# Sixty-four tokens at a time: re-tiling a delta-rule recurrence that runs beside a feed-forward

## The chip, the cores and the metric

One Trainium2 chip, of which the kernel uses one core. The metric is device time in microseconds (us): the median of repeated executions. The engines are named as in the profile: PE (matmul) with PEld (its weight loads), DVE (vector), ACT (scalar), POOL, and SP, whose queue issues the DMAs. Each engine works through its own queue in the order in which the program issued the instructions.

## The reference, cut to what matters

A delta-rule attention over 4 batches, 8 heads, 768 tokens and a head size of 48, followed by a feed-forward with SiLU (384 to 2048 to 384) on the 3072 tokens.

```python
k_n = k / (np.linalg.norm(k, axis=-1, keepdims=True) + 1e-06)
state = np.zeros((B, H, D, D))
for t in range(S):
    kt, vt, bt = k_n[:, :, t], v[:, :, t], beta[:, :, t, None]
    y[:, :, t] = np.einsum('bhd,bhde->bhe', q[:, :, t], state)
    v_old = np.einsum('bhde,bhd->bhe', state, kt)
    state = state + bt[:, :, :, None] * np.einsum('bhd,bhe->bhde', kt, vt - v_old)
x = y.transpose(0, 2, 1, 3).reshape(B * S, H * D)
h = x @ w_in
out = (h * (1 / (1 + np.exp(-h)))) @ w_out
```

The weights arrive as 64-bit floats and are narrowed to 32 bits on the chip.

## The kernel before, in words

**Chunks and units.** The 768 tokens are cut into 6 chunks of 128. A unit is one batch of one chunk: 128 tokens on the 128 partitions, all 8 heads beside one another. So a chunk has four units.

**Attention of a chunk** has three parts.

- `prepare` (L889): for each unit, `turn` (L353) transposes keys and queries (tile `kq`, groups `pt`), and `score` (L376) multiplies keys with keys and with queries (L387, banks `pa`, 128x128 per head); ACT (L397) and DVE (L403, with the mask `above`) scale and mask the result into `ap`. `block_out` and `block_in` bring the 32x32 diagonal blocks of `ap` through DRAM into the tile `g`, one block to a partition. `scale` and `size` are POOL's work on keys and values.
- `invert` (L441): DVE inverts all 32x32 blocks of a chunk at once, two instructions for each of 30 steps (L465, L469); the inverses go through DRAM into `xe` and `xi`.
- `solve` (L508): `merge` (L526) makes inverses of 64x64 from those of 32x32. `keys` (L551) subtracts from the values what the state holds for the keys. `inner`, `across` (L567, L577) solve first for tokens 0 to 63 (partitions `lo`), then carry over to tokens 64 to 127 (`hi`), then solve these; `keep` copies results to `z`. `old` (L600) and `new` (L627) add up the output of old state and new tokens in a bank `pyc`, `update` (L609) adds to the state. Every batch has a state tile, moved once per chunk. Four units run through these steps as a pipeline, shifted by one. The output leaves a bank by copies of ACT and DVE in turn (L681) and, for odd heads, through the tile `part` and DMAs into `xT`.

**Feed-forward of a chunk** runs for two batches at a time (256 tokens): `hidden` (L724) is `xT` times `w_in` (L730, banks `phid`) with SiLU by ACT into `gT` (L740); then, for the first chunk, `project` (L748) multiplies with `w_out` (L753, `po`), and for the others `combine` (L810) does so with seven smaller products (L824, `px` and `py`) on sums of operands that DVE makes (`sum_g`, `sum_w`). It is a generator: every `go(pieces)` emits one piece, 1.3 to 1.5 us of matmuls.

**What sets the order.** `pin` (L88) fixes the order on each engine to the order of emission, `in_line` (L98) that of the DMAs on SP. The driver at the end of the kernel interleaves by hand: pieces of the feed-forward of chunk c are emitted between the steps of preparation, inversion and solution of chunk c + 1. `squares` and `norms` (L284, L301) make the next chunk's scale factors on ACT and DVE during `solve`.

**The start.** Nothing overlaps chunk 0's attention but the narrowing of the weights, 8 pieces of `w_in` and 8 of `w_out`: `narrow` (L150) has two steps on ACT (L158, L163), three on DVE (L160, L166, L170) and one on POOL (L174) for a piece. `fill(n)` emits n of the DVE steps, `until(piece)` all up to a piece. `busy` (L261) emits filler matmuls that touch nothing.

Of the kernel before, what the change touches and what calls it, by code (L numbers as in the profile page):

```python
# [21 lines left out]
def kernel(  # L22
# [84 lines left out]
    N = len(units)  # L107
    NK = NBK = NZ = B
# [9 lines left out]
    def chunk_of(src, i):  # L118
        b, c = units[i]
        return src[b, :, c * C : (c + 1) * C, :].rearrange("h t d -> t h d")  # L120

    def load_k(i):
        if i < N:
            in_line(nc.sync.dma_start(out=packed(kbufs[i % NK]), in_=chunk_of(k, i)))

    def load_q(i):
        if i < N:
            in_line(nc.sync.dma_start(out=packed(zbufs[i % NZ]), in_=chunk_of(q, i)))

    def load_v(i):  # L130
        if i < N and i not in vfs:
            vfs[i] = load.tile([P, H, D], FP32, name="vf", bufs=4)
            in_line(nc.sync.dma_start(out=vfs[i][:], in_=chunk_of(v, i)))
# [5 lines left out]
    states = [const.tile([P, NP, 2 * W], FP32, name=f"state{b}") for b in range(B)]  # L139
    pin(nc.vector.memset(states[B - 1][:], 0.0))  # L140
    beta_fm = mlp.tile([BH, S], FP32, name="beta_fm", tag="gT", bufs=3)
    in_line(nc.sync.dma_start(out=beta_fm[:], in_=beta.rearrange("b h s -> (b h) s")))
    for load_one in (load_k, load_q):
        for i in range(B):
            load_one(i)
# [107 lines left out]
    for t in states[: B - 1]:  # L253
        nc.gpsimd.memset(t[:], 0.0)

    HH = HB * H
# [4 lines left out]
    def busy(after=None, how=NoSync):  # L261

        pw = bank(psC, "c", "pw")
        done = pin(nc.tensor.matmul(
            pw[:, 0:DM], lhsT=ident[:],
            rhs=states[B - 1][:].rearrange("p a w -> p (a w)")[:, 0:DM], start=True, stop=True,
        ))
        if after is not None:
            behind(done, after, how)
        return done  # L270
# [5 lines left out]
    def beta_of(c):  # L276
        pb = bank(psA, "a", "pb")
        pin(nc.tensor.transpose(pb[:, 0:BH], beta_fm[:, c * C : (c + 1) * C], ident[0:BH, 0:BH]))
        pin(nc.scalar.activation(out=beta_tok[:, c, :], in_=pb[:, 0:BH], func=ACTF.Copy))
# [4 lines left out]
    def squares(c):  # L284

        sums[c] = small.tile([P, BH], FP32, name="ss", bufs=1)[:]
        for b in range(B):
            if c == 1:
                sq = packed(zbufs[b])
            else:  # L290
                if b % HB == 0:
                    two = work.tile([P, HB, H, D], FP32, name="sq", tag="g" if c > 0 else "xg"[b // HB], bufs=1)
                sq = two[:, b % HB]
            pin(nc.scalar.activation(
                out=sq, in_=packed(kbufs[(c * B + b) % NK]), func=ACTF.Square
            ))
            pin(nc.vector.tensor_reduce(
                out=sums[c][:, b * H : (b + 1) * H], in_=sq, axis=AX.X, op=ALU.add
            ))
# [45 lines left out]
    def size(i):  # L345
# [3 lines left out]
            out=vfs[i][:], in0=vfs[i][:],  # L349
# [25 lines left out]

    def score(i, u, rooms):  # L376

        b, c = units[i]
        kq, bt = u["kq"], steps[c][:, b * H : (b + 1) * H]
        ap = work.tile([P, H, 2, C], FP32, name="ap", tag="ap", bufs=4)  # L380
        u["ap"] = ap
        for g, room in enumerate(rooms):
            pa = [bank(*room, f"pa{e}") for e in range(2)]
            for pp in range(2):
                for e in range(2):
                    rows = slice(W * e, W * e + D)
                    u["last"] = pin(nc.tensor.matmul(  # L387
                        pa[e][:, pp * 2 * C : (pp + 1) * 2 * C],
                        lhsT=kq[rows, 2 * g + pp, 0, :],
                        rhs=kq[rows, 2 * g + pp, :, :].rearrange("p j t -> p (j t)"),  # L390
                        start=True, stop=True,
                    ))
            for e in range(2):
                heads = [(4 * g + 2 * pp + e, 2 * C * pp) for pp in range(2)]
                by_act = 2 - e
                for h, at in heads[:by_act]:
                    copied = pin(nc.scalar.activation(  # L397
                        out=ap[:, h, 0, :], in_=pa[e][:, at : at + C], func=ACTF.Copy,
                        scale=bt[:, h : h + 1],
                    ))  # L400
                for n, (h, at) in enumerate(heads):
                    j = 1 if n < by_act else 0
                    masked = pin(nc.vector.scalar_tensor_tensor(  # L403
                        out=ap[:, h, j:2, :],
                        in0=pa[e][:, at + j * C : at + 2 * C].rearrange(
                            "p (j t) -> p j t", j=2 - j
                        ),
                        scalar=bt[:, h : h + 1],
                        in1=above[:].unsqueeze(1).to_broadcast([P, 2 - j, C]),
                        op0=ALU.mult, op1=ALU.mult,  # L410
                    ))
            u["ends"] = (copied, masked)
            yield

    def block_out(i, u):
# [13 lines left out]
        for j in range(NB):  # L429
            rows = slice(T * j, T * (j + 1))  # L430
            in_line(nc.sync.dma_start(
                out=there[b, :, j].rearrange("h s t -> s h t"), in_=ap[rows, :, 0, rows]
# [8 lines left out]
    def invert(c):  # L441
# [41 lines left out]
        if c == 0:  # L483
            xe = sum_room[:, B * SLAB : B * SLAB + BH * T]
# [23 lines left out]
    def solve(c, us):  # L508
# [3 lines left out]
        lo, hi = slice(0, W), slice(W, P)  # L512
        A, CC = (psA, "a"), (psC, "c")
        vs = {x: vfs.pop(c * B + x) for x in range(B)}
        pzs, pys = {}, {}
        xe = xes.pop(c)

        def z_of(x):
            return zbufs[x]

        if c == 0:
            pin(nc.gpsimd.memset(sum_room[:, 0 : B * SLAB], 0.0))
            slab = {x: sum_room[:, x * SLAB : (x + 1) * SLAB] for x in range(B)}
        y = work.tile([P, 2, HH, T], FP32, name="y", tag="g", bufs=1)

        def merge(g, second):  # L526
# [3 lines left out]
            for n in range(HB):  # L530
                x = g * HB + n
                for h in range(H):
                    for k in range(2):
                        even, odd = slice(W * k, W * k + T), slice(W * k + T, W * (k + 1))
                        if second:
                            to, left, right = even, y[odd, g, n * H + h, :], xis[g][odd, n * H + h, T:W]
                        else:
                            to, left, right = odd, us[x]["ap"][even, h, 0, odd], xe[even, x * H + h, :]
                        at = T * (n * H + h)
# [4 lines left out]
            if second:  # L544
                pin(nc.scalar.copy(xis[g][0:T, :, T:W], pm[0:T]))
                pin(nc.vector.tensor_copy(out=xis[g][W : W + T, :, T:W], in_=pm[W : W + T]))
            else:
                pin(nc.scalar.copy(y[T:W, g], pm[T:W]))
                pin(nc.vector.tensor_copy(out=y[W + T : P, g], in_=pm[W + T : P]))

        def keys(x):  # L551

            ph = bank(*CC, "ph")
            for p in range(NP):
                st = states[x][:, p, :].rearrange("p (e w) -> p e w", e=2)[:, :, 0:D]
                pin(nc.tensor.matmul(  # L556
                    ph[:, 2 * D * p : 2 * D * (p + 1)], lhsT=us[x]["kq"][:, p, 0, :], rhs=st,
                    start=(p == 0), stop=True, skip_group_check=True,
                ))
            add(x, slice(0, P), ph[:, 0:DM].rearrange("p (h d) -> p h d", h=H))  # L560

        def add(x, rows, what):
            pin(nc.vector.tensor_tensor(  # L563
                out=vs[x][rows], in0=vs[x][rows], in1=what[rows], op=ALU.add
            ))

        def inner(x, rows):  # L567

            if rows == lo:
                pzs[x] = bank(*CC, "pz")[:, 0:DM].rearrange("p (h d) -> p h d", h=H)  # L570
            for h in range(H):
                yield pin(nc.tensor.matmul(  # L572
                    pzs[x][rows, h, :], lhsT=xis[x // HB][rows, x % HB * H + h, :],
                    rhs=vs[x][rows, h, :], start=True, stop=True,
                ))

        def across(x):  # L577

            for h in range(H):
                yield pin(nc.tensor.matmul(  # L580
                    pzs[x][hi, h, :], lhsT=us[x]["ap"][lo, h, 0, W:C],
                    rhs=z_of(x)[lo, h // 2, h % 2, 0:D], start=True, stop=True,
                ))

        def together(*rows):
            for _ in zip_longest(*rows):
                pass

        def keep(x, rows):
            pin(nc.scalar.copy(  # L590
                z_of(x)[rows, :, :, 0:D], pzs[x][rows].rearrange("p (a e) d -> p a e d", e=2)
            ))
            if c == 0:
                to = slab[x][rows, D:].rearrange("p (g w) -> p g w", g=2)[:, :, 0 : 2 * (D + GAP)]
                pin(nc.scalar.copy(
                    to.rearrange("p g (h w) -> p g h w", h=2)[:, :, :, 0:D],
                    pzs[x][rows].rearrange("p (g h) d -> p g h d", g=2)[:, :, 1:3, :],
                ))

        def old(x):  # L600

            pys[x] = bank(*A, "pyc")
            for p in range(NP if c > 0 else 0):
                pin(nc.tensor.matmul(  # L604
                    pys[x][:, C * p : C * (p + 1)], lhsT=states[x][:, p, :],
                    rhs=us[x]["kq"][:, p, 1, :], start=(p == 0), stop=False, skip_group_check=True,
                ))

        def update(x):  # L609
            if c == NCH - 1:  # L610
# [492 lines left out]
```

## Time and profile before

| | before |
|---|---|
| median of 3 runs | 766.16 us (765.92 to 770.08) |
| span of the profiled execution | 766.0 us |
| PE busy | 730.7 us (95%) |
| DVE busy | 420.2 us (55%) |
| ACT busy | 247.2 us (32%) |
| POOL busy | 84.4 us (11%) |
| first matmul of the feed-forward | 93.43 us |
| feed-forward of chunk 1 begins | 222.5 us |
| feed-forward of chunk 5 begins | 684.43 us |

The profile is of one execution; its span begins with its first instruction, and the time of a run and the span differ by 0.02% here. Busy time is not time on the path: matmuls are pipelined, so the pace of a group of matmuls is read from the start of one group to the start of the next.

### The profile page before, as it was taken

The page shows a single profiled execution, that of the slowest core. Times are in us where ns is not written, and L with a number is a line of the kernel's source. Part 1 is how long each engine was busy: PE and PEld are TensorE (multiplying, and loading weights), DVE is VectorE, ACT ScalarE, POOL GpSimd, SP SyncE. Part 2 cuts the span into 40 slices and gives each one's busy share as a digit, 9 for nine tenths or more (in the row PEclk, how much of TensorE's full clock was granted, in tenths as well). Part 3 has the DMA queues.
Part 4 walks back from the last instruction along what each step waited for, and adds up shares of the span by engine and source line. Part 5 has one row for each costly group of instructions (what it writes and reads, how often), then busy time and mean ns, then how long its engine had stood idle before and what let it go on. Part 6 is the DMA issues. An engine that isn't in the chain of part 4 may idle for free.

```text
span 766.0 us, 16569 instructions
## 1 busy us (share of the span) xinstructions
PE 730.7 (95%) x6806; PEld 631.0 (82%) x6806; DVE 420.2 (55%) x1090; ACT 247.2 (32%) x552; POOL 84.4 (11%) x95
## 2 busy tenths in 40 slices
PE   7489899899999999999999999999999999999998
PEld 5256687477778999898999988999987999999987
DVE  6889687872445853555763455673455672321212
ACT  5434466121444122434112434212425212322020
POOL 4005337100021000030000021000012000000000
PEclk9779799999999999999999999999999999999999
DMA  9797445131154022144012044122043013010000
GB/s 176 147 202 218 140 148 109 35 89 20 28 102 79 16 85 34 22 106 80 18 76 43 20 104 78 23 77 43 8 95 67 15 49 70 8 37 1 21 1 21
DMA packets 156283, 51.91 MB, mean 68 GB/s; under 512 B 141840, under 2 KB 148752, under 8 KB 156208
## 3 DMA queue, kind: packets, MB, share of 16 engines
q1 hardware_dynamic: 156208, 50.85, 29.0%
q8 instruction: 54, 0.88, 0.5%
q14 instruction: 21, 0.17, 0.1%
HBM read 34.70 MB, written 14.16 MB: 64 GB/s over the span
## 4 chain that ended last, share of the span: by engine, by line
PE 81%; DVE 10%; DMA 3%; ACT 2%; issue 2%; SPq 1%; POOL 1%; ACTq 0%; DVEq 0%
PE phid L730 31%; PE px L824 13%; PE py L824 11%; PE pa L387 5%; PE pz L572 4%; PE po L753 3%; DVE x L469 3%; DVE rank L465 3%; PE ph L556 2%; PE pt L364 2%; PE pyc L632 2%; PE py L540 2%; PE px L540 2%; PE pyc L604 1%; PE pu L615 1%
## 5 line engine op out<-in xcount | busy, mean ns | idle before, releaser
L730 PE MATMUL phid<-xT,w_in 128*128 128x256 f32 x1152 | 260.7, 382 | 2.2 <-ACT gT L740 1.6
L730 PEld LDWEIGHTS phid<-xT,w_in 128*128 128x128 f32 x1152 | 215.0, 190 | 37.0 <-issue 6.3
L740 ACT ACTIVATE gT<-phid 128x512 f32<-128x512 f32 x96 | 57.2, 597 | 188.7 <-PE phid L730 148.3
L403 DVE SCALAR_TENSOR_TENSOR ap<-pa,g,above 128x128 f32<-128x128 f32 x192 | 58.1, 376 | 41.6 <-ACT ap L397 41.6
L469 DVE TENSOR_TENSOR x<-x,rank 128x30 f32<-128x30 f32 (+9 forms) x180 | 59.7, 332 | 7.4 <-ACT x L458 1.1
L465 DVE TENSOR_TENSOR rank<-g,x 128x30 f32<-128x30 f32 (+9 forms) x180 | 59.4, 330 | 5.0
L806 DVE TENSOR_TENSOR sums_of_g<-gT 128x384 f32<-128x384 f32 (+1 forms) x60 | 29.3, 510 | 58.3 <-ACT gT L740 47.5
L824 PE MATMUL py<-w_out,sums_of_g 128*128 128x192 f32 x320 | 56.8, 329 | 0.0
L824 PE MATMUL px<-sums_of_w,sums_of_g 128*128 128x192 f32 x320 | 56.8, 329 | 0.0
L824 PEld LDWEIGHTS px<-sums_of_w,sums_of_g 128*128 128x128 f32 x320 | 52.2, 190 | 1.4 <-issue 1.4
L824 PEld LDWEIGHTS py<-w_out,sums_of_g 128*128 128x128 f32 x320 | 52.2, 190 | 0.4
L397 ACT ACTIVATE ap<-pa,g 128x128 f32<-128x128 f32 x144 | 41.5, 368 | 30.7 <-PE pa L387 29.7
L426 POOL MEMSET x<- 128x1024 f32 x6 | 5.7, 952 | 405.0 <-DMA xT<-part 403.5
L387 PE MATMUL pa<-kq 48*128 48x256 f32 x384 | 49.7, 390 | 0.2 <-DVE ap L403 0.2
L572 PEld LDWEIGHTS pz<-vf,xi 64*64 64x64 f32 x768 | 38.1, 142 | 13.3 <-issue 7.3
L753 PE MATMUL po<-w_out,gT 128*128 128x384 f32 x128 | 44.7, 495 | 2.9 <-POOL w_out L174 2.9
L572 PE MATMUL pz<-vf,xi 64*64 64x48 f32 x768 | 42.7, 227 | 4.9 <-DVE vf L563 4.4
L387 PEld LDWEIGHTS pa<-kq 48*128 48x128 f32 x384 | 36.2, 186 | 11.5 <-issue 7.8
L563 DVE TENSOR_TENSOR vf<-vf,ph 128x384 f32<-128x384 f32 x20 | 11.1, 554 | 53.1 <-PE ph L556 53.1
L753 PEld LDWEIGHTS po<-w_out,gT 128*128 128x128 f32 x128 | 23.4, 190 | 18.4 <-POOL w_out L174 4.1
L590 ACT COPY z<-pz 64x384 f32<-64x384 f32 x48 | 22.6, 472 | 46.2 <-PE pz L572 40.1
L563 DVE TENSOR_TENSOR vf<-vf,pz 64x384 f32<-64x384 f32 x24 | 13.4, 557 | 42.1 <-PE pz L580 26.1
(134 smaller groups left out, 955.4 us busy)
## 6 DMA issues: line engine op xcount, KB each, us to landing
kb<-in_k_dram SPq DMA_DIRECT2D x24, 192.0 KB, 3.1
z<-in_q_dram SPq DMA_DIRECT2D x24, 192.0 KB, 3.7
vf<-in_v_dram SPq DMA_DIRECT2D x24, 192.0 KB, 3.9
out_dram<-o SPq DMA_DIRECT2D x24, 192.0 KB, 2.0
w_out<-in_moe_w_in_dram SPq DMA_DIRECT2D x4, 768.0 KB, 6.3
blocks<-ap SPq DMA_DIRECT2D x96, 32.0 KB, 1.7
g<-blocks SPq DMA_DIRECT2D x24, 128.0 KB, 2.5
up<-x SPq DMA_DIRECT2D x6, 512.0 KB, 2.6
```

The costliest lines, as they stand in the source:

```text
L387: u["last"] = pin(nc.tensor.matmul(pa[e][:, pp * 2 * C : (pp + 1) * 2 * C], lhsT=kq[rows, 2 * g + pp, 0, :], rhs=kq[rows, 2 * g + pp, :, : ...
L397: copied = pin(nc.scalar.activation(out=ap[:, h, 0, :], in_=pa[e][:, at : at + C], func=ACTF.Copy, scale=bt[:, h : h + 1],))
L403: masked = pin(nc.vector.scalar_tensor_tensor(out=ap[:, h, j:2, :], in0=pa[e][:, at + j * C : at + 2 * C].rearrange("p (j t) -> p j t", j= ...
L465: pin(nc.vector.tensor_tensor(out=tv, in0=g[:, 0:m, m : m + 1].to_broadcast([P, m, n]), in1=x[:, m : m + 1, m + 1 : T].to_broadcast([P, m, ...
L469: yield pin(nc.vector.tensor_tensor(out=x[:, 0:m, m + 1 : T], in0=x[:, 0:m, m + 1 : T], in1=tv, op=ALU.add))
L540: pin(nc.tensor.matmul(pm[to, at : at + T], lhsT=left, rhs=right, start=True, stop=True))
L572: yield pin(nc.tensor.matmul(pzs[x][rows, h, :], lhsT=xis[x // HB][rows, x % HB * H + h, :], rhs=vs[x][rows, h, :], start=True, stop=True,))
L730: pin(nc.tensor.matmul(ph[:, j * GT : (j + 1) * GT], lhsT=w_in[:, a, (2 * f + j) * P : (2 * f + j + 1) * P], rhs=xTs[c, hf][:, a, :], star ...
L740: pin(nc.scalar.activation(out=gTs[f // FG][:, f % FG, :], in_=ph[:], func=ACTF.Silu, scale=0.5))
L753: pin(nc.tensor.matmul(po[:, 0:DM], lhsT=gTs[f // 2 // FG][:, f // 2 % FG, at : at + C], rhs=w_outs[f // HFF][:, f % HFF, :], start=(f == ...
L806: pin(nc.vector.tensor_tensor(out=sums_of_g[:, k, fs], in0=of[0], in1=of[1], op=op))
L824: pin(nc.tensor.matmul(to, lhsT=at, rhs=quarter(f, *b) if isinstance(b, tuple) else sums_of_w[b][:, f], start=start and f == 0, stop=f == ...
```

## The change

A unit is now 64 tokens of two batches, one batch on partitions 0 to 63, the other on 64 to 127 (`fetch`: two DMAs per unit and tensor; the first ones on two queues). A chunk is still 128 tokens and four units: number 2s + g holds the chunk's half s of batches 2g and 2g + 1. Scores are made only within 64 tokens, in 64x64 pieces; the step `across` is gone, and the state is moved after each 64 tokens (two times per chunk) instead. All products of the recurrence are written as 64x64 tiles of the array, in the order (0,0), (1,1), (0,1), (1,0) of row half and column half. Scaling and masking the scores becomes one multiplication by a mask per pair of banks; the mask is made ahead by POOL (`weigh`). Feed-forward inputs `xT` now belong to a half s of the chunk for all four batches. The first half of chunk 0 needs no state, so its feed-forward is emitted before the second half is solved. The driver's order for the start is rewritten, that of the later chunks is as before.

The diff, cut to its core (`halves` are the two partition halves):

```diff
+    halves = [slice(0, W), slice(W, P)]
+    def fetch(to, src, i, early=False):
+        n, c = units[i]
+        at = c * C + W * (n // 2)
+        for r, rows in enumerate(halves):
+            of = src[2 * (n % 2) + r, :, at : at + W, :].rearrange("h t d -> t h d")
+            if early and r == 1:
+                pin(nc.scalar.dma_start(out=to[rows], in_=of))
+            else:
+                in_line(nc.sync.dma_start(out=to[rows], in_=of))
...
+    def weigh(i):
+        m = work.tile([P, H, W], FP32, name="mask")
+        pin(nc.gpsimd.tensor_tensor(out=m[:], in0=causal..., in1=steps..., op=ALU.mult))
     def score(i, u, rooms):
-        ap = work.tile([P, H, 2, C], FP32, name="ap", tag="ap", bufs=4)
+        ap = work.tile([P, H, 2, W], FP32, name="ap", tag="ap", bufs=4)
+        for p in range(NP):
+            for r, cols in enumerate(halves):
+                for e in range(2):
+                    pin(nc.tensor.matmul(pa[e][cols, C * p : C * (p + 1)]...,
+                        lhsT=kq[rows, p, 0, cols], rhs=kq[rows, p, :, cols], ...))
+        for e in range(2):
+            heads = slice(e, H, 2)
+            pin(nc.vector.tensor_tensor(out=ap[:, heads], in0=pa[e]..., in1=m[:, heads]..., op=ALU.mult))
...
     def solve(c, us):
+        def tiles():
+            for g in range(2):
+                for p in range(NP):
+                    for r, e in ((0, 0), (1, 1), (0, 1), (1, 0)):
+                        yield g, p, r, e
+        def keys(s): ...    # 32 matmuls 64x64, two additions to the values on DVE
+        def inner(s, g): ...    # 16 matmuls 64x64 in two tiles, then ACT copies to z
+        def old(s): ...     # 32 matmuls, banks pyc of two partition halves
+        def update(s): ...  # 32 matmuls, two additions to the states on DVE
+        def new(s): ...     # 32 matmuls
+        def leave(s):
+            part = work.tile([P, 2, NP, C], FP32, name="part", tag="x", bufs=1)
+            ...             # two copies to part, twelve to xT, ACT and DVE in turn
-        for k in range(B + 3): ...   # the pipeline of four units
+        if c == 0:
+            merge(0, False); yield; merge(0, True); yield
+            inner(0, 0); inner(0, 1); yield
+            first_new(); yield; update(0); yield
+            merge(1, False); yield; merge(1, True)
+        else:
+            merge(0, False); merge(1, False); yield
+            merge(0, True); merge(1, True); keys(0); yield
+            old(0); inner(0, 0); inner(0, 1); yield
+            update(0); yield
+            new(0); leave(0)
+        keys(1); yield
+        old(1); inner(1, 0); inner(1, 1); yield
+        update(1); yield
+        new(1); leave(1); yield
...
+    def store(c, s, r, o):      # two DMAs for one before
...
     (feed_forward of chunk 0, first half:)
+            both = [project(c, b, o) for b in range(hf * HB, (hf + 1) * HB)]
+            if hf == 0:
+                for _ in zip(*both):
+                    yield
+            yield from chained(*both)
...
     (driver, start)
-    squares(1)
-    norms(1)
...
-    fill(3)
+    fill(9)
...
-    for n, _ in enumerate(solve(0, us)):
-        fill(2)
-        ...
+    chain = solve(0, us)
+    for n in range(4):
+        go(chain)
+        fill(1)
+        for _ in range(3):
+            busy()
+    for i in (2, 3, 7):
+        more(i)
+    for n, piece in enumerate((4, 4, 4, 5, 5, 5, 6, 7)):
+        until(("in", piece))
+        go(pieces, 2)
+        if n >= 1:
+            go(chain)
+    more(6)
     ...
-    for n in range(4):
-        go(prep)
-        go(pieces, 3 if n < 2 else 2)
-        fill(6 if n == 0 else 3)
+    for n in range(8):
+        until(("out", n))
+        if n == 0:
+            squares(1)
+            norms(1)
+        if n == 1:
+            more(5)
+        go(pieces)
+        go(prep)
+    go(prep, 99)
     inv = invert(1)
-    for n in range(20):
+    for n in range(16):
         go(inv, 2)
         go(pieces)
```

`more(i)` issues the load of piece i of `w_out`. In the loop over n, `prep` emits in turn the scores of a unit and the transposes of the next.

## The prediction

> **What bounds the kernel now.** I read the stretches of the timeline first: which engine is full in which stage.
>
> ```profile
> 94.00:137.00 43.00, 42.48 (x279) 32.41 (x277) 32.87 (x60) 26.53 (x53) 23.69 (x18) 1.00 0.48 127
> 137.00:165.00 28.00, 23.97 (x89) 16.75 (x90) 24.57 (x68) 4.68 (x9) 2.37 (x2) 1.00 0.14 42
> ...
> 339.00:455.00 116.00, 115.05 (x1151) 104.18 (x1150) 63.84 (x182) 35.87 (x85) 6.40 (x8) 1.00 0.25 55
> ```
>
> The columns are length, then busy time of PE, weight load, DVE, ACT and POOL, then clock and DMA. From 94 us on PE is full but for 4 us near 140, and a period of the steady part (one chunk's feed-forward with the next chunk's attention, 116.4 us, four of them from 222.5 to 684.4) holds 1 us of PE idleness. So PE time counts there; how PE's attention groups run in one period is the second view (start and length in us; a group's pace is the distance to the next start):
>
> ```profile
> 340.16 2.00 PE L387 MATMUL pa<-kq 48*128 48x256 f32 x16
> 342.09 1.56 PE L730 MATMUL phid<-xT,w_in 128*128 128x256 f32 x6
> ...
> 406.95 3.71 PE L556 MATMUL ph<-state,kq 128*128 128x96 f32 x32
> 410.50 1.49 PE L730 MATMUL phid<-xT,w_in 128*128 128x256 f32 x6
> ...
> 421.79 1.13 PE L572 MATMUL pz<-vf,xi 64*64 64x48 f32 x16
> 422.85 1.57 PE L824 MATMUL px<-sums_of_w,gT 128*128 128x192 f32 x8
> ...
> 431.44 0.67 PE L615 MATMUL pu<-z,bkb 128*64 128x48 f32 x16
> 431.94 1.06 PE L632 MATMUL pyc<-ap,z 128*64 128x128 f32 x16
> 432.93 1.57 PE L824 MATMUL px<-sums_of_w,sums_of_g 128*128 128x192 f32 x8
> ```
>
> Every matmul leaves two records. Before 222.5 us DVE matters too: it inverts blocks and narrows the 16 weight pieces, three operations each (the timeline of DVE), with 1.83 us of POOL behind them (L174):
>
> ```profile
> 98.74 0.56 DVE L160 TENSOR_SCALAR w_out<-w_out 128x768 f32<-128x768 f32 x1
> 99.33 0.56 DVE L166 TENSOR_SCALAR w_out<-w_out 128x768 uint32<-128x768 uint32 x1
> 99.93 0.96 DVE L170 SCALAR_TENSOR_TENSOR w_out<-w_out,w_out 128x768 uint32<-128x768 uint32 x1
> ```
>
> Here PE's clock also falls when PE idles (stretches of 5 us, the clock third from the end):
>
> ```profile
> 25.00:30.00 5.00, 0.63 (x5) 0.26 (x3) 4.11 (x4) 1.52 (x2) 1.88 (x1) 1.00 0.38 80
> 30.00:35.00 5.00, 1.46 (x6) 1.00 (x6) 2.78 (x14) 1.80 (x8) 0.00 (x0) 0.56 1.30 178
> ```
>
> **1. PE work per chunk.** Scores: 4 units x 1.93 = 7.72 us. They become 128 records of 128 columns over four 64x64 quadrants. Nearest row: L632, 16 records in 0.99 us, 62 ns each with two tiles side by side, so 124 ns per tile and 31 ns with four: 4.0 us. The other products become 128 records each over four quadrants (inner: two). One 64x64 tile alone takes 1.06/16 = 66 ns per record; from 426.91 to 427.98 three tiles pass 48 records, 22 ns each, so tiles overlap fully. Four give 16.5 ns: 2.1 us; the merges issue 128 records in 2.14 us, so the queue can feed that. No row shows four quadrants: the dear bound is two at a time, 33 ns, the cheap one 16.5, and I take the latter because three tiles already scale. Keys 3.55 to 2.1, old 3.92 to 2.1, update 2.0 to 2.1, new 3.96 to 2.1, inner with across 6.39 to 128 x 33 = 4.2. Sum 27.5 to 16.6: 10.9 us less. By the dear bound it is 7.9 + 4 x 4.2 + 4.2 = 29.
>
> The Trainium skill (TensorEngine Tiling, Key Properties) says that changing the tiling mode drains the array, which speaks against a finer mode. The row: six phid take 1.30 us in a row and 1.40 to 1.49 beside a switch, 0.1 to 0.2 us; the groups per period hardly change in number, so by row and rule alike the sum stays.
>
> **2. New waits in a steady period.** Old(1) needs a bank that leave(0) still reads: two part copies of 0.58, then twelve in which ACT (0.26) and DVE (0.28) alternate on a bank, returned 3.2 us after new(0); keys(1) and one piece cover 2.5. PE waits 0.7, and 0.6 more for the keys' two additions (0.56 each) queued behind these copies. Later DVE stands in the order squares, states, sums, norms (3.5 us, 15 operations), leave(1)'s copies; ACT alternates with these copies, and behind it stands the eviction of px, without which PE's next chain can't start. After inner(1): 1.4 + 0.35 + 3.2 + 1.15 + 1.36 + 3.5 + 2.0 + 0.35 = 13.3 us, over 9.4 us of PE work: 3.9 us of wait. The 0.95 us at 441 goes. A period saves 10.9 + 0.95 - 0.7 - 0.6 - 3.9 = 6.6 us; the fourth (no norms, half an update left where four were skipped) 8.7. Together 28 us, bounds 12 (twice the waits) and 45 (none).
>
> Off the path in these periods: the scores' evictions, two DVE operations of 512 columns (about 0.7 us each: a 128x512 copy, L373, takes 0.68, a 128x384 addition 0.55) for eight of DVE and six of ACT; the masks, 128x512 on POOL at 0.906 us per 384 columns, so 1.2 us, which with the two scalings of 0.83 fit a unit's 4.7 us; and the loads, now two DMAs of half the size per unit. SP issues one in 0.39 us, twelve more per chunk; the four for k stand between the block transfers that the inversion waits for, 1.78 + 0.31 + 2 x 0.39 = 2.9 us of SP in a unit's 4.7, so they hide there, and without that cover the inversion would start 1.6 us later. At the very end stand four stores for two, 0.62 us each to issue: 0.6 us more after what can overlap.
>
> **3. Start.** First scores: 1.4 us a unit for 2.9, the mask queue on POOL in front, so the inversion begins 4.5 us earlier (31.7 to 27.2), and with it the loads that follow. But ACT reads weight piece 5 ahead of the xi copy; that piece is queued on SP behind the inversion's twelve loads and lands about 67.3. Then 0.9 + 0.6 + 0.7 to the first inner at 69.8, 2.1 inner, 1.8 first product, 2.0 of filler twice (the last hides the xT copies), 2.6 for a halved clock: feed-forward starts near 80.3, for 93.4.
>
> PE work from there to the next feed-forward: phid 41.5, po 44.5, scores 4.1, turns 1.8, rest of solve(0) 9.6, solve(1) 17.1, switches 4: 122.6 us. Alone, that ends at 203.
>
> The changed order of issue puts the narrowing of a piece just before its use, on DVE behind state work that itself waits for PE. ("In 6" is piece 6 of w_in, "out 0" piece 0 of w_out.) In-order queues make this a loop: PE's phid or po waits for POOL's last addition on the piece, the piece waits on DVE behind an operation that needs an earlier PE group, and behind the waiting matmul stand new(1), the scores and everything later on PE. So PE waits: in 6, state additions 1.2 + 2.4 + 1.85: 5.5 us. In 7, behind leave(1)'s copies 3.6 + 2.4 + 1.85: 7.9. Out 0, ACT behind the last gT, 0.7 + 1.0 + 1.85: 3.6. Out 1 stands behind gT 0.7, ACT's two steps 1.9, squares 3.2, norms 3.5, the mask 1.2, the score 1.5, then its own 2.4 + 1.85: 16.3 us after the last phid, of which 3.6 (out 0) and 3.8 (po, pa) are spent: 8.9. Out 2, 4, 6: PE scores, DVE 1.5, narrowing 2.4, POOL 1.85: 5.8 each. Out 3 and 5: ACT's low half queues behind the kq copies, 0.1 + 1.2 + 1.0 + 1.85: 4.2 each. Solve(1): 1.5. Sum 53 us. That is the largest term and shown by no row; its bounds are 20 (if half of the queues overlap better than I read) and 65. Before, the same narrowing ran ahead of PE's needs, and cost the 4 us near 140.
>
> The clock: it fell to 0.5 at 30.7 after 5 us idle, and came back at 47.8 after 5.8 us of nearly steady work that began at 42. So each of six gaps over 5 us (in 6, in 7, out 1, 2, 4, 6) makes the next some 5 us of work 2.5 slower: 15 us, bounds 0 and 20.
>
> By the Trainium skill (TensorE: Matmul & The Clock Gate, the HAM clock gate) an idle window of about 3.4 us halves the clock and one busy window restores it; an estimate by it is 1.7 us a gap, 10 us in all, and 5 us off my total.
>
> So 80.3 + 122.6 + 53 + 15 = 271 for 222.5: 48 us more. Sum against the profiled 766.0 us, which is the median (766.16) within 0.02%: 766 - 28 + 0.6 + 48 = 787.
>
> **Rivals.** *The start pays off* (0.15): narrowing runs ahead because DVE has some 17 us free between 80 and 105, and PE waits about 10 us in all. Start ends at 213, total 766 - 9 - 28 + 1 = 730. For it: PE already has its work 13 us earlier. Against: queues are strictly ordered. The sides change where waits and clock together make 47 us rather than 68. *The clock stays full* (0.15): 787 - 15 = 772. For it: 4 us idle near 140 left it at 1.00. *Quadrants go two at a time* (0.07): 29 us of PE for 27.5 and the waits stay, so four periods lose 5.8 each where they saved 28: 787 + 28 + 23 + about 16 at the start = 854.
>
> **How the numbers follow.** The forecast has 0.63 and centres on 787; 752 to 808 takes in the clock rival, twice or none of the steady waits, and part of the way to the first rival, leaving out most of that and the third. Differences under 0.5% (3.8 us) can't be told from none. Faster 0.19 (the first rival and the low end of the clock's), same 0.10, slower 0.71.
>
> **What would show it.** Right: phid first near 80; idle PE before phid with releaser POOL w_in, before po with POOL w_out, over 35 us in all; clock 0.5 between 105 and 195; second feed-forward after 250; steady period near 110; pa near 31 ns and keys near 17 ns a record; a PE wait for the px eviction in three periods. Wrong: a second feed-forward before 225, periods over 114, or keys over 25 ns a record.

## The result, and the profile after

The changed kernel takes 809.04 us (median of 4 runs, 808.57 to 813.2) against 767.72 us (4 runs) before: ratio 1.0546, 95% interval 1.0511 to 1.0581. It is slower, as forecast, but by 41 us where the forecast said 21, and 1 us above the range. Ratios, here and below, compare fast executions alone (left out as slow: one each of e1, 766.14 us, e2, 1554.3, and e8, 747.95, and one of the kernel before, 942.95), while medians are of all. The profiled execution has a span of 807.3 us, 41.3 more than before. By stages, in us:

| | before | after | difference | forecast |
|---|---|---|---|---|
| first matmul of the feed-forward | 93.43 | 84.58 | -8.9 | -13.1 |
| feed-forward of chunk 1 begins | 221.48 | 274.83 | +53.4 | +48 |
| four steady periods after that | 462.8 | 448.9 | -13.9 | -28 |
| last feed-forward and tail | 81.7 | 83.6 | +1.8 | +0.6 |

A feed-forward that overlaps a preparation begins here, and in all runs below, with the start of the transposes in front of its first phid, in the timeline of PE. The 222.5 and 684.43 of the earlier table are the first phid of chunks 1 and 5 as the chain of work counts them, from the end of the group ahead; the timeline has 222.35 and 684.27.

The stretches after (length, busy time of PE, weight load, DVE, ACT, POOL, then clock, DMA share, GB/s):

```profile
85.00:110.00 25.00, 24.46 (x519) 20.86 (x517) 3.92 (x8) 6.68 (x12) 1.11 (x1) 1.00 0.19 74
110.00:210.00 100.00, 52.88 (x297) 31.65 (x298) 43.15 (x69) 23.22 (x37) 31.11 (x24) 0.73 0.22 49
275.00:397.00 122.00, 109.01 (x1469) 98.77 (x1468) 61.47 (x162) 28.41 (x63) 15.68 (x19) 0.94 0.29 60
398.00:509.00 111.00, 106.33 (x1467) 95.80 (x1466) 56.47 (x149) 26.94 (x57) 11.08 (x14) 0.98 0.28 59
```

Between 110 and 210 us PE is busy half the time, at a clock of 0.73; before, it was full from 94 us on but for 4 us. DVE, ACT and POOL are not full either, so PE seems to wait on an order, not on capacity (e1 tests this). The first steady period (third line) has PE idle for 13 us, the second for 4.7. Who ends PE's longest waits (us in total, times, longest):

```profile
PE po L787 <- POOL w_out L185: 34.4, 7, 6.8
PE phid L759 <- POOL w_in L185: 13.3, 2, 7.9
...
PE px L857 <- ACT o L886: 9.9, 3, 3.3
PE px L857 <- ACT gT L769: 7.2, 1, 7.2
...
PE pa L416 <- DVE kq L390: 2.0, 1, 2.0
```

One turn of the loop in the start, the wait for piece 1 of `w_out`, in the timeline of three engines (start, length, engine, and in brackets the idle time before and its releaser):

```profile
141.47 1.15 PE L416 MATMUL pa<-kq 48*64 48x128 f32 x32
142.75 1.29 DVE L423 TENSOR_TENSOR ap<-pa,mask 128x512 f32<-128x512 f32 x2 [1.35 <-PE pa L416]
143.96 0.86 DVE L171 TENSOR_SCALAR w_out<-w_out 128x768 f32<-128x768 f32 x1
144.86 1.06 DVE L177 TENSOR_SCALAR w_out<-w_out 128x768 uint32<-128x768 uint32 x1
145.95 1.47 DVE L181 SCALAR_TENSOR_TENSOR w_out<-w_out,w_out 128x768 uint32<-128x768 uint32 x1
147.56 1.82 POOL L185 TENSOR_TENSOR w_out<-w_out,w_out 128x768 int32<-128x768 int32 x1 [0.96 <-DVE w_out L181]
149.44 5.49 PE L787 MATMUL po<-w_out,gT 128*128 128x384 f32 x8 [6.82 <-POOL w_out L185]
```

PE makes scores, DVE evicts them, only then narrows the piece, POOL adds, and PE, idle all the while, goes on at half speed: 5.49 us for the eight records that take 2.85 at full clock.

The attention's groups in a steady period (the pace is the distance to the next start):

```profile
586.03 1.11 PE L613 MATMUL pyc<-kq,state 48*48 48x64 f32 x64
586.96 2.03 PE L589 MATMUL pz<-vf,xi 64*64 64x48 f32 x64
588.91 1.57 PE L857 MATMUL px<-w_out,gT 128*128 128x192 f32 x8
...
591.71 1.15 PE L625 MATMUL pu<-z,bkb 64*64 64x48 f32 x64
592.79 1.57 PE L857 MATMUL px<-sums_of_w,gT 128*128 128x192 f32 x8
594.29 1.11 PE L635 MATMUL pyc<-ap,z 64*48 64x64 f32 x64
595.22 1.10 PE L576 MATMUL ph<-state,kq 48*64 48x48 f32 x64
596.25 1.57 PE L857 MATMUL py<-w_out,sums_of_g 128*128 128x192 f32 x8
...
621.76 1.10 PE L416 MATMUL pa<-kq 48*64 48x128 f32 x32
622.80 1.56 PE L759 MATMUL phid<-xT,w_in 128*128 128x256 f32 x6
```

64 records over four quadrants take 0.93 to 1.08 us (14.5 to 17 ns each), over two 1.95 us (30 ns), scores 1.04 us for 32 (32.5 ns).

What is new against the forecast is the first steady period. The timeline of SP, DVE, ACT and PE there (SPq is SP's queue of DMA issues):

```profile
274.16 6.28 SPq L695 DMA_DIRECT2D xT<-part  x10
280.54 3.21 SPq L129 DMA_DIRECT2D z<-in_q_dram  x4
283.84 1.22 SPq L780 DMA_DIRECT2D out_dram<-o  x2
285.15 5.46 SPq L129 DMA_DIRECT2D vf<-in_v_dram  x8
290.71 2.05 SPq L444 DMA_DIRECT2D blocks<-ap  x4
...
312.05 0.36 DVE L469 COPY x<-g 128x16 f32<-128x16 f32 x3 [14.75 <-DMA g<-blocks]
312.27 0.60 ACT L471 COPY x<-g 128x128 f32<-128x128 f32 x2 [10.64 <-DMA kb<-in_k_dram]
312.78 1.08 ACT L769 ACTIVATE gT<-phid 128x512 f32<-128x512 f32 x2
313.42 5.49 PE L857 MATMUL px<-w_out,gT 128*128 128x192 f32 x16 [7.25 <-ACT gT L769]
```

SP issues 24 transfers before the first block transfer of the inversion; ACT reaches the inversion's first copy long before its data, and two gT that PE needs stand behind it. The first unit's scores were ready in ap at 281.62 us, so its block transfers, from 290.71 on, waited for the queue. Before the change less stood there, and the first block transfer came 6.6 us after the period's start, where it now comes 15.9 us after it:

```profile
218.27 3.87 SPq L678 DMA_DIRECT2D xT<-part  x5
222.24 0.53 SPq L128 DMA_DIRECT2D z<-in_q_dram  x1
222.88 3.41 SPq L133 DMA_DIRECT2D vf<-in_v_dram  x4
226.41 0.63 SPq L760 DMA_DIRECT2D out_dram<-o  x1
228.07 1.99 SPq L431 DMA_DIRECT2D blocks<-ap  x4
```

### The profile page after: what moved, and what is told of

It is laid out like the page before. It is cut to its first block, busy times and chain, and to the rows that moved or that the text cites. A ratio compares the mean times of both kernels' runs of the same rounds, so it can differ in the third digit from the quotient of the medians.

```text
span 807.3 us, 20074 instructions
## 1 busy us (share of the span) xinstructions
PE 702.1 (87%) x8702; PEld 598.7 (74%) x8702; DVE 382.0 (47%) x916; ACT 194.0 (24%) x387; POOL 105.7 (13%) x118
## 4 chain that ended last, share of the span: by engine, by line
PE 48%; DVE 6%; DMA 2%; ACT 2%; SPq 1%; issue 1%; DVEq 0%; ACTq 0%
PE phid L759 20%; PE px L857 12%; PE py L857 8%; PE pz L589 2%; PE pa L416 1%; PE pt L381 1%; DVE xT L698 1%; PE px L554 1%; DVE sums_of_g L839 1%; PE py L554 1%; DMA blocks<-ap 1%; DVE x L482 1%; PE pyc L635 1%; DVE rank L478 1%; DVE ss L314 1%
## 5 line engine op out<-in xcount | busy, mean ns | idle before, releaser
L787 PE MATMUL po<-w_out,gT 128*128 128x384 f32 x128 | 60.8, 632 | 34.4 <-POOL w_out L185 34.4
L398 POOL TENSOR_TENSOR mask<-causal,g 128x512 f32<-128x512 f32 x24 | 25.1, 1056 | 376.9 <-DVE g L343 357.3
L423 DVE TENSOR_TENSOR ap<-pa,mask 128x512 f32<-128x512 f32 x48 | 30.8, 686 | 72.9 <-PE pa L416 66.2
L857 PE MATMUL px<-w_out,gT 128*128 128x192 f32 x160 | 31.5, 350 | 7.2 <-ACT gT L769 7.2
L857 PEld LDWEIGHTS px<-w_out,gT 128*128 128x128 f32 x160 | 28.7, 204 | 8.6 <-ACT gT L769 8.0
L630 DVE TENSOR_TENSOR state<-state,pu 128x384 f32<-128x384 f32 x22 | 11.2, 549 | 49.4 <-PE pu L625 49.4
L275 PE MATMUL pw<-state,ident 128*128 128x384 f32 x78 | 31.3, 556 | 3.0 <-POOL xi L270 3.0
L698 DVE COPY xT<-pyc 16x128 f32<-16x128 f32 (+1 forms) x66 | 19.2, 291 | 27.7 <-ACT part L680 25.4
L416 PEld LDWEIGHTS pa<-kq 48*64 48x64 f32 x768 | 21.9, 140 | 11.9 <-issue 9.2
L589 PE MATMUL pz<-vf,xi 64*64 64x48 f32 x768 | 27.8, 225 | 3.0 <-issue 2.2
## 6 DMA issues: line engine op xcount, KB each, us to landing
g<-blocks SPq DMA_DIRECT2D x24, 128.0 KB, 2.3
```

What stands on the lines that cost most here:

```text
L275: done = pin(nc.tensor.matmul(pw[:, 0:DM], lhsT=ident[:], rhs=states[1][:].rearrange("p g a d -> p (g a d)"), start=True, stop=True,))
L416: pin(nc.tensor.matmul(pa[e][cols, C * p : C * (p + 1)].rearrange("p (j t) -> p j t", j=2), lhsT=kq[rows, p, 0, cols], rhs=kq[rows, p, :, ...
L423: pin(nc.vector.tensor_tensor(out=ap[:, heads], in0=pa[e][:].rearrange("p (a j t) -> p a j t", a=NP, j=2), in1=m[:, heads].unsqueeze(2).to ...
L589: pin(nc.tensor.matmul(pzs[s, g][rows, h, :], lhsT=xis[s][rows, g * H + h, :], rhs=vs[s][rows, g, h, :], start=True, stop=True, skip_group ...
L698: pin(engine(to.rearrange("p (g t) -> p g t", g=2), py[at : at + n, h // 2]))
L787: pin(nc.tensor.matmul(po[:, 0:DM], lhsT=gTs[f // 2 // FG][:, f // 2 % FG, at : at + C], rhs=w_outs[f // HFF][:, f % HFF, :], start=(f == ...
```

## The experiments

Theory: the 53 us of the start are an order of issue, a loop of in-order queues over DVE, POOL and PE, with the halved clock that follows each gap; the steady part gains less than forecast because of two more queues, SP's and DVE's. Rivals: the narrowing needs that time in any order; the slow groups are slow for another reason; the new tiles cost more than they save.

**e1: narrowing emitted ahead.** One or two pieces before the matmuls that use them.

```diff
-    for n, piece in enumerate((4, 4, 4, 5, 5, 5, 6, 7)):
-        until(("in", piece))
+    for n, piece in enumerate((("in", 5), ("in", 6), ("in", 6), ("in", 7),
+                               ("in", 7), ("out", 0), ("out", 1), ("out", 1))):
+        until(piece)
...
+    more(5)
     more(6)
...
-        until(("out", n))
+        until(("out", min(7, n + 2)))
...
-        if n == 1:
-            more(5)
```

> The changed kernel with one edit: in the start each narrowing step is emitted one or two pieces ahead of the matmuls that use it. Theory (order of issue): the waits of phid and po for POOL's last addition (13.3 and 34.4 us in the changed kernel) fall below 10 us together, the halved clock between 105 and 205 us goes with them (about 17 us), the second feed-forward begins near 215 us instead of 274.8, and the time is near 750 us (740 to 762). Rival (capacity: DVE, ACT and POOL need this time for the pieces whatever the order): the waits move to other pieces but stay over 30 us, and the time is above 785 us.

757.49 us, ratio to before 0.9847 (0.9801 to 0.9894): 1.5% below before. The second feed-forward begins at 223.53. PE's waits there:

```profile
PE po L787 <- POOL w_out L185: 10.1, 3, 9.1
```

phid waits for POOL no more. The same work by the same engines, in another order, gives back 51 of the 53 us, so capacity is ruled out. The wait of 9.1 us that is left is for piece 3: POOL's addition on it stands behind `size`, which waits for v, eight loads that SP issues in 9.2 us.

**e2 and e2b: filler in the gaps.** `busy()` matmuls in front of each group that waits; order and narrowing as changed.

```diff
         until(("in", piece))
+        for _ in range({6: 14, 7: 21}.get(n, 0)):   # e2b: 7 and 10
+            busy()
         go(pieces, 2)
...
+        for _ in range((9, 18, 15, 9, 15, 9, 15, 0)[n]):   # e2b: (4, 9, 7, 4, 7, 4, 7, 0)
+            busy()
         go(pieces)
```

> The changed kernel with filler matmuls in front of the groups that wait for a narrowed piece; order and narrowing are untouched. Theory (the clock falls because PE idles): the waiting groups start when they did, but phid of 12 records takes 2.86 us again instead of 4.3 to 4.5, po of 8 records 2.85 instead of 5.49, and the time falls by about 17 us to 792 us (786 to 798). Rival (these groups are slow for another reason, such as their operands' memory being written at that time): their lengths stay, and the time is 809 us or, by fillers that overrun, more.

830.32 us. The fillers were twice as long as planned, and this run does not tell the theories apart.

> As e2, with half as many filler matmuls: one leaves two records of 0.37 us each, 0.73 us together, so e2's 125 took 91 us and overran waits and slow groups of 65 us (809 + 26 = 835, measured 830). The 59 here take 43 us, inside the waits. Theory (clock falls because PE idles): po of 8 records back near 2.85 us, phid of 12 near 2.86, time near 793 us (787 to 800). Rival (slow for another reason): lengths stay at 4.3 to 5.5, time 807 us or more.

799.98 us, ratio 1.0443 (1.0393 to 1.0493), 9 us less than the changed kernel; the second feed-forward begins at 261.09 for 274.83. In the timeline of PE:

```profile
149.88 4.78 PE L275 MATMUL pw<-state,ident 128*128 128x384 f32 x14
155.63 2.85 PE L787 MATMUL po<-w_out,gT 128*128 128x384 f32 x8 [0.96 <-POOL w_out L185]
```

Useless work in front makes the same group take 2.85 us for 4.66. Only the group of piece 1, where 3.33 us of gap were left, stayed slow (4.54). So the groups were slow because PE had been idle. The size is 14 us in the start, and the total shows 9 of it.

**e3: squares and norms ahead of the solution.**

```diff
+    squares(c + 2)        # moved here from n == 5
+    norms(c + 2)          # moved here from n == 6
     for n, _ in enumerate(solve(c + 1, us)):
```

> The changed kernel with the squares and norms of the next chunk emitted ahead of the solution instead of between its update and the second output. Theory (the px eviction of ACT stands behind output copies that alternate with DVE, and DVE behind the norms): the three waits of px for o (9.9 us) and the halved clock after two of them (3.6 us) go, with part of the 2 us before pa at 277; time near 796 us (793 to 801). Rival (the output copies alone hold the eviction): more than 2 us of each of the three waits stay, and the time is 804 us or more.

829.14 us, ratio 1.0792 (1.0764 to 1.082): 20 us slower than the changed kernel. The three waits of px for o are gone, as the theory had it, but the time is not: in PE's waits the one for gT is now there three times, and one for y has come:

```profile
PE px L857 <- ACT gT L769: 13.8, 3, 5.9
...
PE px L554 <- DVE y L563: 12.4, 4, 3.4
```

Squares and norms keep DVE from 354.2 to 360.4 us, and the merge's copy of y, which PE needs next, stands behind them. The work has to stand behind what PE waits for, not ahead of it.

**e3b: norms behind the output copies and the first turn.**

```diff
-                if n == 6 and c + 2 < NCH:
-                    norms(c + 2)
...
             us.append(list(turn(i, A, CC))[0])
+            if b == 0 and c > 1:
+                norms(c)
             weigh(i)
```

> The changed kernel with the norms of chunks 2 to 5 put behind the output copies and behind the first turn of the next preparation, squares where they were. e3 traded the px wait for a wait of the merge for DVE's copy of y, which stood behind the squares there. Theory (3.5 us of norms on DVE in the chain leave-copies, px eviction): the px wait is 13.3 - 3.5 = 9.8 us of chain over 9.4 us of PE work, so 0 to 0.5 us are left of 3.3, three times, and the halved clock after two of them goes; the 2 us before pa at 277 shrink too; time near 796 us (792 to 800). Rival (the copies alone hold it): over 2 us stay in each of three periods, time 804 or more.

806.87 us, ratio 1.0535 (1.0487 to 1.0583), not apart from the changed kernel's. The waits of px for o are gone altogether, so the norms were their cause; but the wait for gT, once 7.2 us, is now there in all three periods:

```profile
PE px L857 <- ACT gT L769: 13.0, 3, 7.3
```

The later norms and masks are not what makes the inversion late: in the second period the first scores were ready at 398.21 us (the line of DVE below, two instructions), and their block transfers were issued from 401.01 on, because SP issued almost without a break from 382.33 on. It is again SP's queue. The px wait and the slow clock behind it had been its cover, and without them the period ahead is 5.0 us shorter (117.71 for 122.72).

```profile
396.92 1.29 DVE L423 TENSOR_TENSOR ap<-pa,mask 128x512 f32<-128x512 f32 x2 [1.22 <-POOL mask L398]
```

One wait was changed for another.

**e4: ten transfers of the first half to POOL's queue.**

```diff
-    in_line(nc.sync.dma_start(out=to, in_=part[...]))
+    if c == 1 and s == 0:
+        pin(nc.gpsimd.dma_start(out=to, in_=part[...]))
+    else:
+        in_line(nc.sync.dma_start(out=to, in_=part[...]))
```

> The changed kernel with ten of the small transfers from part to xT (first half of chunk 1 only) issued from POOL's queue instead of SP's. Theory (in the first steady period SP's queue of 27 us holds up the block transfers, so the inversion starts at 312 us and ACT's gT behind it): the inversion starts about 7 us earlier, the wait of px for gT (7.25 us) and the halved clock after it (2.7 us) go; time near 799 us (796 to 803). Rival (the block transfers follow the scores and POOL's masks, not the queue): the wait stays over 5 us, the time within 3 us of 809.

810.01 us, ratio 1.0547 (1.0512 to 1.0583): no change, wait for gT 7.6 us. I had moved the wrong ones: SP was through with the first half at 264.6 us and then stood idle until leave(1)'s copy was ready at 273.9. What counts is issued after that.

**e4b: loads of k and v and the sizes behind the block transfers.**

```diff
             scale(i)
-            load_k(i + B)
-            size(i)
             yield
+        for i in range(c * B, (c + 1) * B): load_k(i + B)
+        for i in range(c * B, (c + 1) * B): load_v(i)
+        for i in range(c * B, (c + 1) * B): size(i)
```

> The changed kernel with the loads of k for the next chunk, the loads of v and POOL's sizes put behind all four units' block transfers in the preparation of chunks 2 to 5. e4 moved transfers of the first half, which were done before leave(1) began; 16.4 us of SP work stand between leave(1) and the first block transfer, and 5.2 us pass per unit after that. Theory (SP's queue in front of and between the block transfers sets the inversion's start): 5.5 us of v loads and 3 x 1.3 us of k loads go from in front of the last one, the inversion of chunk 2 starts near 303 instead of 312 us, the wait of px for gT and the halved clock after it go, 10 us, time near 799 us (796 to 802). Rival (scores or masks set it): the wait stays over 4 us, time 806 or more.

804.76 us, ratio 1.0497 (1.0457 to 1.0536), which overlaps that of the changed kernel, so the times alone would not decide. The trace does: the first block transfer moves from 290.71 to 284.19, the inversion's first copy on ACT from 312.27 to 301.62, and PE no longer waits for gT:

```profile
284.19 2.04 SPq L444 DMA_DIRECT2D blocks<-ap  x4
...
299.58 5.50 SPq L129 DMA_DIRECT2D kb<-in_k_dram  x8
```

The first period takes 114.67 us for 122.72. The wait of 2.0 us before the scores is still there, so it is not SP's: DVE makes the norms until 276.34 us in the changed kernel, then leave(1)'s copies, and only then the copy of kq that these scores read.

**e5: order of the quadrants.**

```diff
-    for r, e in ((0, 0), (1, 1), (0, 1), (1, 0)):
+    for r, e in ((0, 0), (0, 1), (1, 0), (1, 1)):
```

> The changed kernel with the four quadrants of keys, old, update and new in the order (0,0), (0,1), (1,0), (1,1) instead of (0,0), (1,1), (0,1), (1,0): neighbours share a row half. Theory A (four quadrants overlap whatever their order, the pace is that of issue): a group of 64 records stays at 1.05 to 1.15 us, time 809. Theory B (neighbours that share a row half wait for each other, so two at a time): groups of 64 records take 1.6 to 2.1 us, and about 38 such groups add 20 to 40 us: 830 to 850.

812.05 us (2 runs), ratio 1.0593 (1.0546 to 1.0639), not apart from the changed kernel. In the timeline of PE the groups are as they were:

```profile
369.38 1.15 PE L625 MATMUL pu<-z,bkb 64*64 64x48 f32 x64
...
371.95 1.11 PE L635 MATMUL pyc<-ap,z 64*48 64x64 f32 x64
372.88 1.10 PE L576 MATMUL ph<-state,kq 48*64 48x48 f32 x64
```

Four quadrants overlap in this order too (0.93 us from pyc to ph).

**e6: the start in the old order.** The driver's start as before the change, all else as changed.

```diff
-    chain = solve(0, us)
...
-        until(("in", piece))
...
+    for n, _ in enumerate(solve(0, us)):
+        fill(2)
...
+        if n >= 7:
+            go(pieces, 2)
```

> The changed kernel with the order of the start as before the change (all of chunk 0 solved with narrowing steps between, then the feed-forward, narrowing two pieces ahead); tiles, units and later chunks as changed. Theory (the new order of the start costs the time, the new tiles do not): the waits of PE for w_in and w_out are under 8 us, the second feed-forward begins by 215 us (it had 222.5 before, with 11 us more of PE work per chunk), and the time is near 742 us (735 to 757). Rival (the halves solved one behind the other make the start longer by themselves): the second feed-forward begins after 235 us, the time is above 768.

765.51 us, ratio 0.9979 (0.9948 to 1.0011): no change against before. So the new order of the start costs 43.5 us, and the new tiles and units together neither gain nor lose with the old one. This lies between the two theories: the waits for narrowed pieces are gone, but the second feed-forward begins at 233.18, for PE has two other waits:

```profile
PE pa L416 <- ACT kq L386: 13.8, 1, 13.8
...
PE pt L381 <- DMA z<-in_q_dram: 11.3, 2, 6.8
```

Of the second line, 6.8 us belong to chunk 0, where the changed kernel has 5.9; the other 4.5 are new. The first line, in the timeline of POOL and ACT: `size` waits 7.86 us for v until 130.3, POOL's additions follow, that on piece 5 last (140.0 to 141.8); ACT's first step on piece 6 writes where piece 5's raw data lay and waits 14.26 us for it, until 141.88, and the copy of kq stands behind this.

**e7: e1, e4b (in chunk 1 too) and e3b together.**

> The changed kernel with narrowing emitted ahead (e1), k and v loads and sizes behind the block transfers in every preparation (e4b, now in chunk 1 too) and the norms behind the output copies and the first turn (e3b). Theory (three separate causes, each found above, that add up; e3b's masks come later, but the shorter queue of e4b gives them the 9 us): second feed-forward near 212 us, periods near 107 to 109 us, no wait of px for o or gT over 1 us, time near 722 us (714 to 734). Rival (the later masks hold the block transfers, so the inversion and gT stay late as in e3b): gT waits over 2 us in the periods, periods over 111 us, time over 738.

743.51 us, ratio 0.9695 (0.9658 to 0.9732): 3% faster than before, but 22 us over the expectation, some 9 of them in the start and 6 in the three periods. Periods are 108.97, 110.98 and 110.37 us, without any wait of px for o or gT: with a shorter queue of SP, e3b's later masks cost no wait for gT. But the second feed-forward begins at 221.15, not 212, and a wait of 5.5 us for piece 3 and 5.6 us for the inversion's transfers stay in the start:

```profile
PE po L787 <- POOL w_out L185: 6.6, 3, 5.5
...
PE py L554 <- DMA xe<-low: 5.6, 4, 4.2
```

**e8 and e9: eight buffers for queries**, in e7 and in e6 with e4b's and e3b's edits. The queries of the next chunk are now loaded in its predecessor's preparation, behind k.

```diff
-    NK = NBK = NZ = B
+    NK = NBK = B
+    NZ = 2 * B
...
-            return zbufs[2 * s + g]
+            return zbufs[(c * B + 2 * s + g) % NZ]
...
-            for g in range(2):
-                load_q((c + 1) * B + 2 * s + g)
...
+            for i in range(c * B, (c + 1) * B):
+                load_q(i + B)
```

> e7 with eight buffers for queries instead of four, so that the queries of the next chunk are loaded at the end of a preparation and no longer behind leave() of the solution whose results use the same buffers. Theory (in e7 the start still waits on things behind these loads: the 5.5 us before po at 131 and the inversion's late end, 5.6 us of waits for xe): second feed-forward near 215 instead of 221 us, time near 736 us (731 to 741). Rival (query loads bind nothing with narrowing ahead; eight more buffers change only the start's memsets): second feed-forward at 220 or later, time 742 or more.

742.86 us, ratio 0.9641 (0.9589 to 0.9693), not apart from e7. The start lost 6 us (second feed-forward at 227.59; the 5.5 us are still there), the second and third period gained 2 to 3 (107.67 and 108.43): the rival holds for the start.

> e6 (order of the start as before the change) with e4b's and e3b's edits and eight query buffers. In e6 PE waited 4.5 us before a turn and 13.9 us before scores, both in chunk 1's third and fourth unit, whose queries could only be loaded after leave(1) of chunk 0. Theory (that buffer reuse is what the units of 64 tokens cost in the old order): both waits fall below 2 us, second feed-forward by 215 us instead of 233, time near 732 us (725 to 740). Rival (the queue of leave's transfers, not the buffers, is late): a wait over 8 us stays, second feed-forward after 225, time over 745.

748.61 us, ratio 0.9758 (0.9718 to 0.9798). The wait of 4.5 us before the turn, for queries, is gone; the buffers are the likely reason, but e4b's and e3b's edits came with them and are not told apart. Of the 13.8 us for kq 11.9 stay, so that wait was not the buffers. Behind it is again ACT's step on piece 6, which waits 12.45 us for POOL.

## Why the prediction was right and where it was wrong

**The start was right**, by its steps. Waits forecast and measured: piece 6 of `w_in` 5.5 and 5.4 us, piece 7 7.9 and 7.9; `w_out` 0 3.6 and 3.5, 1 8.9 and 6.8, 2, 4 and 6 5.8 and 5.7 each, 3 and 5 4.2 and 3.5; solve(1) 1.5 and 2.9. Together 53 and 50.6. The halved clock cost 17 us (sum of the lengths of po and phid over 2.85 and 2.86) for 15, and that this is close is in part luck: the six gaps over 5 us that were charged cost 11.7, and two gaps of 3.5 us (before `w_out` 0 and 5), charged nothing, cost 5.3. PE work from first to second feed-forward is what is left, 190.2 - 50.6 - 17 = 122.6 us, as forecast. The only miss is the first phid, 84.6 for 80.3: piece 5 landed at 71.7 us, not 67.3, and the copy of xi on ACT stood behind it as foreseen. It makes 4 of the 20 us that the total missed. e1 and e2b show the two causes apart; the rival that the start pays off failed, since strictly ordered queues did keep DVE's free time from being used.

**PE's work was right.** A period without its waits is 105.3 to 105.7 us, 10 less than the 115.5 before, for 10.9 forecast. Two quadrants at a time is ruled out by the trace (14.5 to 17 ns a record, 30 for two), in either order (e5).

**The step that failed is the steady periods' saving** (part 2): 13.9 us for 28, next to the lower bound of 12, which stood for twice the waits. The px wait (3.3 for 3.9 us) and old(1) (0.4 for 0.7) are as forecast. Three terms are missing, the first by far the largest:

- The queue of SP in the first period, 9.9 us: 7.25 of wait for gT, and 2.7 of halved clock after it. The prediction costed the twelve more loads per chunk as hidden in a unit's 4.7 us, with 1.6 us if not, and looked only at the k loads between the block transfers. It did not count what stands in front of the first one: after leave(1) ten small transfers, four of queries, two stores and eight of v, 16.2 us, where before five, one, one and four took 8.4. Later periods hide this, because there 13 us (384.5 to 397.55 in the next one) of feed-forward and px wait lie between new(1) and the next period; after the first chunk there is one po, 1.4 us. A unit also took 5.2 us, not 4.7. e4b removed this wait and the slow clock behind it; e3b shows the same queue in the later periods once their cover is shorter.
- The queue of DVE in the first period, 2.0 us before the scores: norms and leave(1)'s copies ahead of the copy of kq. The prediction followed this queue to the px eviction alone.
- The halved clock after a px wait: 1.8 us in two of three periods. The prediction charged the clock in the start alone, for gaps over 5 us.

9.9, 2.0 and 3.6 make 15.5 us, for 14 between forecast and measurement; the smaller terms nearly cancel. e3b shows that the px wait was the norms, and that removing it alone only uncovers SP's queue behind it; e7 removes both.

**The tail**: four stores are issued in 2.39 us from 802.25, two had taken 0.81, with nothing beside them; this is 1.6 of the 1.8 us, for 0.6 forecast.

The Trainium skill (TensorE: Matmul & The Clock Gate, What's actually happening) has at least one busy window, about 3.4 us, bring the clock back; with one, an estimate by the page is 1.7 us a gap. Here the eight slow groups of the start cost 1.4 to 2.6 us, 2.1 on average (17 / 8), and four of them passed whole, 5.49 us, at half speed. The measurement decides.

Not tried: which of piece 3's and piece 6's waits in e7 could go by loading piece 5 earlier; and what of e7's missing 22 us lies in the clock.

## What to carry to other kernels

Where engines work through strictly ordered queues, a helper's work emitted just before its use makes PE wait for everything ahead of it on that helper, however idle the helper is on average: emit it one or two uses ahead (51 us here). Before counting a transfer or a small vector step as hidden, write down the whole queue it stands in, from the last thing that had to be waited for, at the place with the least cover, here the first period; and add to each PE gap the slower clock behind it. Taking one wait away shows what was due next, and a wait can be the cover of another (e3b): remove two neighbours together before judging (e7).

## What the hardware showed that was not expected

- Gaps of 3.3 to 3.5 us already halve the clock, though not always: after six such gaps (3.51, 3.52 and 3.49 us before po, three of 3.3 before px) the group behind was slow in four. In the changed kernel the clock also fell near 73.4 us, behind gaps of only 2.18 and 2.24 us that 3.3 us of work parted.
- The order of the four quadrants in the stream makes no difference (e5).
- DVE's narrowing step took 2.07 us instead of 0.56 beside an addition of POOL in the changed kernel (126.36, POOL from 125.98 to 128.0). The Trainium skill (SBUF — State Buffer, Who interferes with whom) describes a pair of ports that one of these engines holds for a whole instruction; the step ended 0.43 us after POOL's, which fits.
